# One transfer for the query weights, a projection in one part, and fillers ahead of it, in a decode kernel with attention and an MLP

## The chip, the cores and the metric

The kernel runs on one core of a Trainium2 chip. The metric is the device time of one execution in microseconds, lower is better. Four executions, spread over four kernels, were about a microsecond longer at a mean granted TensorE clock of 0.978 in place of 1.0. Nothing is read from those, but two of them count as fast by the rule used here and widen the interval of their run; the text says where. The profile's span is about 1.4 us shorter than the time.

## The reference

One token goes through a layer norm, then through two branches that are added to it: an attention with 32 query heads and 8 key/value heads over the last 4096 positions of a cache, and a small gated MLP with a sigmoid gate on its result.

```python
xn = layernorm(x)                                   # 1 x 512
q  = (xn @ wq).reshape(32 heads, 128)               # wq 512 x 4096, 4 MB
k, v = the last 4096 of 65536 positions, 8 heads    # 8 MB each
o  = softmax(q k^T * 128**-0.5) v                   # 4 query heads share one k/v head
A  = o.reshape(4096) @ wo                           # wo 4096 x 512, 4 MB
r  = sigmoid(xn @ w_r)
B  = xn + r * ((silu(xn @ w_gate) * (xn @ w_up)) @ w_down)   # 3 x 1.75 MB
out = x + A + B
```

All in all 30.67 MB are read once for one row of output.

## The kernel before

Each engine has a program of its own, ordered by semaphores. In the profile PE is TensorE, DVE is VectorE, ACT is ScalarE, POOL is GpSimd, and SP is SyncE, which here only issues transfers. All large transfers are issued on SP's queue, in this order: wq in two halves, k, v, gate, up, wo, down (in four pieces). `early` puts an issue ahead of the kernel's opening barrier. The weights are laid out so that each partition reads `kt` consecutive rows of wq: a half is 16 KB per partition, the whole 32 KB.

```python
    wq_sb = nc.alloc_sbuf_tensor("wq_sb", [P, KT, NQ], BF16)      # 128 x 4 x 4096
    KH = KT // 2
    wq_v = A_wq.rearrange("(p kt) n -> p kt n", kt=KT)
    ...
    t_wq = [early(nc.sync, "wq0", wq_sb[:, 0:KH, :], wq_v[:, 0:KH, :])]
    t_x = early(nc.scalar, "x", xrow[:], ...)
    ...
    t_wr = dma(ac, "wr", wr_row[:], ...)                          # 1 KB, on ACT's queue
    t_wq.append(dma(sy, "wq1", wq_sb[:, KH:, :], wq_v[:, KH:, :]))
```

`warm(n)` is n matmuls of zeros, 128 x 512, meant to keep TensorE's clock up; `fill(n)` is 2n of them. `gf` is the MLP's gate factor, spread to all partitions by a small matmul. The q projection is done in two parts, one for each half of wq, each with 16 matmuls in four column groups at a time (by the trace the second half's start in fours within 10 ns, and the fours are 0.215 us apart):

```python
    warm(2)
    PE.need(t_gf, t_ones)
    t_gfp = PE.mark(te.matmul(ps[:, 6, 264:265], lhsT=ones_f[0:1, :], rhs=sml[:, 4:5], ...))
    ...
    for kh in range(2):
        if kh == 1:
            for ch in range(2):                                   # clears the banks of the scores
                te.matmul(sc[:, ch, :], lhsT=zst[:], rhs=zmov[:], start=True, stop=False, ...)
            warm(1)
        PE.need(t_wq[kh], t_ps0)
        for hf in range(2):
            for kt in range(kh * KH, (kh + 1) * KH):
                for c in range(4):
                    ins = te.matmul(ps[32 * c:32 * c + 1, hf, :], lhsT=xnT[:, kt:kt + 1],
                                    rhs=wq_sb[:, kt, (4 * hf + c) * 512:(4 * hf + c + 1) * 512],
                                    start=(kt == 0), stop=(kt == KT - 1), tile_position=(0, 32 * c))
            if kh == 1:
                ...                                               # ACT evicts q
```

Then q is transposed, ten fillers run, and the loop over the eight k heads begins: DVE copies a head's k, TensorE transposes it, DVE and ACT evict it, TensorE multiplies it by q. Softmax, the product with v, and the gate and up projections follow, then 24 fillers, the wo matmuls, and those of down:

```python
    with te.Fori(0, 12):
        fill(1)
    PE.need(t_oT2)
    for k, (j0, j1) in enumerate(wo_chunks):                      # one transfer, 32 matmuls
        PE.need(t_wo[k])
        ...
    for k, (j0, j1) in enumerate(wd_chunks):                      # four transfers, 28 matmuls
        PE.need(t_wd[k])
        ...
```

Of the kernel before, what the change touches and what calls it, by code (L numbers as in the profile page):

```python
# [38 lines left out]
def kernel(  # L39
# [14 lines left out]
    nc = tc.nc  # L54
    P = 128
    D = A_x.shape[2]
    KT = D // P
# [15 lines left out]

    wq_sb = nc.alloc_sbuf_tensor("wq_sb", [P, KT, NQ], BF16)
    xrow = nc.alloc_sbuf_tensor("xrow", [1, D], BF16)
    KH = KT // 2
    wq_v = A_wq.rearrange("(p kt) n -> p kt n", kt=KT)

    ahead, ends_at = {}, {}
# [23 lines left out]
    def early(eng, name, out_, in_):  # L103
        s = nc.alloc_semaphore("d_" + name)
        ins = eng.dma_start(out=out_, in_=in_)
        ins.then_inc(s, 16)
        ahead[ins.ins.name] = ins.ins.engine
        return (s, 16)

    t_wq = [early(nc.sync, "wq0", wq_sb[:, 0:KH, :], wq_v[:, 0:KH, :])]  # L110
    t_x = early(nc.scalar, "x", xrow[:], A_x.rearrange("a b d -> (a b) d"))
    W3, F1, F2, F3 = 2, 2, 1, 1

# [13 lines left out]
    q4 = sb("q4", [P, 2, 512], BF16)  # L127
# [8 lines left out]
    zst = sb("zst", [P, P], BF16)  # L136
    zmov = sb("zmov", [P, 512], BF16)
# [14 lines left out]
    xnT = sb("xnT", [P, KT], BF16)  # L152
# [11 lines left out]
    ps = nc.alloc_psum_tensor("ps", [P, 8, 512], F32)  # L164
    psf = ps[:].rearrange("p a b -> p (a b)")
    tp = ps[:, 0:4, :].bitcast(BF16)
    sc = ps[:, 4:6, :]
# [17 lines left out]
    PE, ACT, DVE, POOL, SP = (Eng(nc, nc.tensor, "pe"), Eng(nc, nc.scalar, "act"), Eng(nc, nc.vector, "dve"),  # L185
                              Eng(nc, nc.gpsimd, "pool"), Eng(nc, nc.sync, "sp"))
    te, ac, ve, gp, sy = nc.tensor, nc.scalar, nc.vector, nc.gpsimd, nc.sync

    def warm(n):
        for _ in range(n):  # L190
            te.matmul(ps[:, 7, :], lhsT=zst[:], rhs=zmov[:], start=True, stop=True)  # L191

    def fill(n):
        warm(2 * n)

    def ends(ins):
        ends_at[ins.ins.engine] = ins.ins.name
        return ins

    def dma(eng, name, out_, in_):  # L200
        s = S("d_" + name)
        ins = eng.dma_start(out=out_, in_=in_)  # L202
        ins.then_inc(s, 16)
        if name == "v0":
            ends(ins)
        return (s, 16)

    t_wr = dma(ac, "wr", wr_row[:], B_w_r.rearrange("(a d) -> a d", a=1))
    t_wq.append(dma(sy, "wq1", wq_sb[:, KH:, :], wq_v[:, KH:, :]))
    TP = W // PH  # L210

    def pair(name, tile_, cache, i0, i1):
# [22 lines left out]
    t_ps0 = DVE.mark(ve.memset(ps[:, 0:2, :].rearrange("p a b -> p (a b)"), 0.0))  # L235
# [17 lines left out]
    for kt in range(KT):  # L253
        ins = te.matmul(ps[:, 6, 256 + kt:257 + kt], lhsT=xn_row[:].rearrange("a (p k) -> a k p", k=KT)[:, kt, :],  # L254
                        rhs=ident_bf[0:1, 0:1], start=True, stop=True)
# [9 lines left out]
    t_identf = DVE.mark(ve.tensor_copy(out=ident_f[:], in_=ident_bf[:]))  # L265
    DVE.need(t_rth)
    t_gf = DVE.mark(ve.tensor_scalar(out=sml[:, 4:5], in0=sml[:, 3:4], scalar1=0.25, scalar2=0.25, op0=ALU.mult, op1=ALU.add))
    warm(2)
    PE.need(t_gf, t_ones)
    t_gfp = PE.mark(te.matmul(ps[:, 6, 264:265], lhsT=ones_f[0:1, :], rhs=sml[:, 4:5], start=True, stop=True))  # L270
    with nc.allow_low_precision(reason="0/1 values are exact in bf16"):
# [4 lines left out]
                                     in_=ident_bf[:].rearrange("p (q h) -> p h q", h=2)))  # L276
# [11 lines left out]
    PE.need(t_xnT)  # L288
    t_qe = []
    t_qpad = []  # L290
    for kh in range(2):
        if kh == 1:
            for ch in range(2):
                te.matmul(sc[:, ch, :], lhsT=zst[:], rhs=zmov[:], start=True, stop=False, skip_group_check=True)
            warm(1)
        PE.need(t_wq[kh], t_ps0)
        for hf in range(2):
            for kt in range(kh * KH, (kh + 1) * KH):
                for c in range(4):
                    ins = te.matmul(ps[32 * c:32 * c + 1, hf, :], lhsT=xnT[:, kt:kt + 1],  # L300
                                    rhs=wq_sb[:, kt, (4 * hf + c) * 512:(4 * hf + c + 1) * 512],
                                    start=(kt == 0), stop=(kt == KT - 1), tile_position=(0, 32 * c))
            if kh == 1:
                t_qp = PE.mark(ins)
                ACT.need(t_qp)
                t_qe.append(ACT.mark(ac.copy(out=q4[:, hf, :], in_=ps[:, hf, :])))  # L306

    def q_out(hf, t_qt):
        DVE.need(t_qt, t_qpad0)
# [5 lines left out]
    for hf in range(2):  # L315
# [3 lines left out]
        for hl in range(4):  # L319
            ins = te.transpose(qT_ps[:, hl, :], q4[:, hf, hl * DH:(hl + 1) * DH], ident_bf[:])  # L320
# [76 lines left out]
    with te.Fori(1, 9) as i:  # L397
# [36 lines left out]
                              start=True, stop=True))  # L434
# [6 lines left out]
    for h in range(2):  # L441
        PE.need(t_p[h])
        for k in range(8):
            ins = te.transpose(tp[:, h, k * P:(k + 1) * P], p_sb[:, h, k * P:(k + 1) * P], ident_bf[:])
# [39 lines left out]
    with te.Fori(1, 9) as i:  # L484
# [4 lines left out]
        for tl in range(4):  # L489
            ins = te.matmul(pv_ps[32 * tl:32 * tl + 32, :], lhsT=pTcur[:, tl].rearrange("p q e r -> p (q e r)"),  # L490
                            rhs=vin[:, 0].rearrange("p (q t) d -> p t q d", t=4)[:, tl],
                            start=True, stop=False, tile_position=(0, 32 * tl))
        ins.then_inc(pe_pva, 1)
        te.wait_ge(s_vb, i)
        for tl in range(4):
            ins = te.matmul(pv_ps[32 * tl:32 * tl + 32, :], lhsT=pTcur[:, 4 + tl].rearrange("p q e r -> p (q e r)"),  # L496
                            rhs=vin[:, 1].rearrange("p (q t) d -> p t q d", t=4)[:, tl],
                            start=False, stop=True, tile_position=(0, 32 * tl))
        ins.then_inc(pe_pv, 1)
        collect(psf[:, bass.ds(4 * 512 + g * 8, 8)]).then_inc(pe_col, 1)  # L500
        for _ in range(W3):
# [10 lines left out]
                               in_=ps[:, 4, 8:72].rearrange("p (g u j) -> p g j u", g=HP, u=2), axis=AX.X))  # L512
# [7 lines left out]
    for m in range(2):  # L520
        PE.need(t_g if m == 0 else t_u)
        for kt in range(KT):
            for c in range(4):
                ins = te.matmul(ps[32 * c:32 * c + 1, 2 + m, 0:FC], lhsT=xnT[:, kt:kt + 1],
                                rhs=wgu[:, m * KT * F + kt * F + c * FC:m * KT * F + kt * F + (c + 1) * FC],
                                start=(kt == 0), stop=(kt == KT - 1), tile_position=(0, 32 * c))
# [18 lines left out]
    def grouped(j, lhsT, w):  # L545
        c = j % 4
        return te.matmul(a_ps[32 * c:32 * c + 1, :], lhsT=lhsT, rhs=w[:, j * D:(j + 1) * D], start=(j < 4), stop=False,  # L547
                         tile_position=(0, 32 * c), skip_group_check=True)

    def by_halves(lhsT, row, start=False, stop=False):  # L550
        for c in range(2):
            ins = te.matmul(g_ps[c], lhsT=lhsT, rhs=row[:, c * HD:(c + 1) * HD], start=start, stop=stop,  # L552
                            tile_position=(0, 32 * c), skip_group_check=True)
        return ins

    for k, (j0, j1) in enumerate(wo_chunks):
        PE.need(t_wo[k])
        for j in range(j0, j1):
            ins = grouped(j, oT2[:, j:j + 1], wo_sb)
# [4 lines left out]
    for k, (j0, j1) in enumerate(wd_chunks):  # L564
        PE.need(t_wd[k])
        for j in range(j0, j1):
            ins = by_halves(hTr[:, j, 0:1], wd_sb[:, j * D:(j + 1) * D], start=(j == 0), stop=(j == FB - 1))
# [42 lines left out]
```

## Time and profile before

| | before |
|---|---|
| time, median of 3 runs | 78.77 us (78.75 to 78.80) |
| span of the profiled run | 77.4 us |
| TensorE, VectorE, ScalarE busy | 73%, 57%, 39% of the span |
| moved from memory | 30.67 MB, 397 GB/s over the span |

The question is which wait ends last. A line of the timeline gives the start in us, how long the group lasted, the engine, the source line, the operation with output and inputs, how many instructions were merged, and in brackets the idle time ahead of it and what ended that.

A second source is used throughout: the trace's records of single DMA packets, each with start, duration and size. The page counts 16 DMA engines, and each of the large transfers has 16 completion writes of 4 bytes in the records (272 for the 17 of the kernel before); I read them as one from each engine when its share is done. The last of the 16 is taken as the landing (for wo in the kernel before it is at 70.52 us, the last of the 16 updates of its semaphore at 70.97, and PE starts at 71.11); the time from the first to the last is called the spread here.

### The profile page before, as it was taken

The page shows a single profiled execution, that of the slowest core. Times are in us where ns is not written, and L with a number is a line of the kernel's source. Part 1 is how long each engine was busy: PE and PEld are TensorE (multiplying, and loading weights), DVE is VectorE, ACT ScalarE, POOL GpSimd, SP SyncE. Part 2 cuts the span into 40 slices and gives each one's busy share as a digit, 9 for nine tenths or more (in the row PEclk, how much of TensorE's full clock was granted, in tenths as well). Part 3 has the DMA queues.
Part 4 walks back from the last instruction along what each step waited for, and adds up shares of the span by engine and source line. Part 5 has one row for each costly group of instructions (what it writes and reads, how often), then busy time and mean ns, then how long its engine had stood idle before and what let it go on. Part 6 is the DMA issues. An engine that isn't in the chain of part 4 may idle for free.

```text
span 77.4 us, 1658 instructions
## 1 busy us (share of the span) xinstructions
PE 56.4 (73%) x634; PEld 29.9 (39%) x652; DVE 43.8 (57%) x96; ACT 30.3 (39%) x41; POOL 10.2 (13%) x22
## 2 busy tenths in 40 slices
PE   0015965676997997997995766788887798872891
PEld 0010411335775685685682225222232254431340
DVE  2764900109956957966963672987989347400212
ACT  2771002301895896797775044333333420000001
POOL 3950000000230210220217700000000000000000
PEclk9999999999999999999999999999999999999999
DMA  5999999999999999999999999999999979969910
GB/s 128 398 416 407 441 457 449 407 415 407 466 449 415 415 415 441 457 441 407 411 415 441 457 432 407 415 451 385 467 385 489 516 305 542 441 291 400 361 41 1
DMA packets 2457, 30.72 MB, mean 397 GB/s; under 512 B 275, under 2 KB 406, under 8 KB 790
## 3 DMA queue, kind: packets, MB, share of 16 engines
q1 hardware_dynamic: 2450, 30.67, 94.0%
q8 instruction: 2, 0.03, 0.2%
q14 instruction: 1, 0.01, 0.0%
q10 hardware_dynamic: 4, 0.00, 0.0%
HBM read 30.67 MB, written 0.00 MB: 397 GB/s over the span
## 4 chain that ended last, share of the span: by engine, by line
DMA 71%; PE 13%; ACT 8%; DVE 3%; issue 1%; SPq 1%
DMA k_sb<-in_B_w_down_dram 51%; DMA k_sb<-in_A_k_cache_dram 20%; ACT kT L352 8%; PE ps L380 7%; PE ps L552 3%; PE ps L389 2%; DVE kin L344 2%; DVE kT L349 1%; SPq L202 1%; DVE kT L575 1%; SPq L84 0%; SPq L101 0%
## 5 line engine op out<-in xcount | busy, mean ns | idle before, releaser
L352 ACT COPY kT<-ps 128x1024 bf16<-128x1024 bf16 x19 | 18.5, 1016 | 9.4 <-PE ps L380 9.4
L380 PE MATMUL ps<-perm_bf,kin 128*128 128x128 bf16 x256 | 17.0, 220 | 1.3 <-DVE kin L344 0.9
L380 PEld LDWEIGHTS ps<-perm_bf,kin 128*128 128x128 bf16 x256 | 14.3, 98 | 5.6 <-issue 4.2
L344 DVE COPY kin<-k_sb 128x2048 bf16<-128x2048 bf16 x16 | 11.0, 690 | 5.4 <-DMA k_sb<-in_A_k_cache_dram 4.7
L191 PE MATMUL ps<-zmov,zst 128*128 128x512 bf16 x27 | 9.9, 397 | 2.3 <-PEq L84 1.2
L349 DVE COPY kT<-ps 128x1024 bf16<-128x1024 bf16 x13 | 9.0, 689 | 2.6 <-PE ps L380 2.2
L475 ACT CAST pvS<-ps 128x512 bf16<-128x512 f32 x8 | 4.7, 585 | 10.0 <-PE ps L481 10.0
L389 PE MATMUL ps<-kT,qAB 128*32 128x512 bf16 x68 | 6.8, 389 | 1.9 <-ACT kT L352 1.9
L337 POOL COPY qAB<-qpad 128x64 bf16<-128x64 bf16 x8 | 3.8, 471 | 31.7 <-PE ps L389 31.7
L191 PEld LDWEIGHTS ps<-zmov,zst 128*128 128x128 bf16 x45 | 4.0, 98 | 5.7 <-issue 2.1
L455 DVE COPY vin<-v_sb 128x2048 bf16<-128x2048 bf16 x8 | 5.5, 684 | 1.1 <-PE ps L490 1.0
L461 DVE COPY vin<-v_sb 128x2048 bf16<-128x2048 bf16 x8 | 5.5, 682 | 0.0
L490 PE MATMUL ps<-vin,pTcur 128*32 128x512 bf16 x32 | 3.2, 386 | 2.6 <-ACT pvS L475 2.2
L576 ACT CAST kT<-ps 1x256 bf16<-1x256 f32 x1 | 0.4, 362 | 11.8 <-PE ps L552 11.8
L502 PE MATMUL ps<-zmov,zst 128*128 128x512 bf16 x16 | 4.7, 376 | 0.0
L562 DVE TENSOR_TENSOR kT<-ps,kT 128x512 f32<-128x512 f32 x1 | 0.7, 692 | 6.4 <-PE ps L547 6.4
L254 PE MATMUL ps<-ident_bf,xn_row 1*128 1x1 bf16 x4 | 0.3, 166 | 5.2 <-DVE xn_row L249 5.2
L300 PE MATMUL ps<-wq_sb,xnT 128*1 128x512 bf16 x32 | 2.9, 500 | 1.4 <-DMA wq_sb<-in_A_wq_dram 1.4
L496 PE MATMUL ps<-vin,pTcur 128*32 128x512 bf16 x32 | 3.2, 387 | 0.3 <-DVE vin L461 0.2
L490 PEld LDWEIGHTS ps<-vin,pTcur 128*32 128x32 bf16 x32 | 1.1, 92 | 6.0 <-DVE vin L455 5.5
L389 PEld LDWEIGHTS ps<-kT,qAB 128*32 128x32 bf16 x68 | 1.9, 92 | 3.9 <-DVE kT L349 1.1
L306 ACT CAST q<-ps 128x512 bf16<-128x512 f32 x2 | 1.1, 588 | 5.5 <-PE ps L300 5.5
(92 smaller groups left out, 51.7 us busy)
## 6 DMA issues: line engine op xcount, KB each, us to landing
k_sb<-in_A_k_cache_dram SPq DMA_DIRECT2D x4, 2048.0 KB, 22.6
v_sb<-in_A_v_cache_dram SPq DMA_DIRECT2D x4, 2048.0 KB, 38.4
wq_sb<-in_A_wq_dram SPq DMA_DIRECT2D x2, 2048.0 KB, 9.3
k_sb<-in_A_wo_dram SPq DMA_DIRECT2D x1, 4096.0 KB, 37.7
wq_sb<-in_B_w_gate_dram SPq DMA_DIRECT2D x1, 1792.0 KB, 43.5
wq_sb<-in_B_w_up_dram SPq DMA_DIRECT2D x1, 1792.0 KB, 47.4
k_sb<-in_B_w_down_dram SPq DMA_DIRECT2D x1, 896.0 KB, 39.5
k_sb<-in_B_w_down_dram SPq DMA_DIRECT2D x1, 512.0 KB, 40.3
```

The source lines that it names most:

```text
L191: te.matmul(ps[:, 7, :], lhsT=zst[:], rhs=zmov[:], start=True, stop=True)
L337: gp.tensor_copy(out=qAB[:], in_=qpad[:, g]).then_inc(s_q, 1)
L344: ve.tensor_copy(out=kin[:, 2 * h:2 * h + 2, :], in_=k_sb[:, g, 2 * h:2 * h + 2, :]).then_inc(s_c[h], 1)
L349: ve.tensor_copy(out=kT[:, b, :], in_=tp[:, b, :]).then_inc(s_ev[b], 1)
L352: ac.copy(out=kT[:, b, :], in_=tp[:, b, :]).then_inc(s_ev[b], 1)
L380: ins = te.transpose(tp[:, b, k * P:(k + 1) * P], kin[:, b, k * P:(k + 1) * P], perm_bf[:])
L389: ins = te.matmul(sc[32 * cq:32 * cq + 32, e, :], lhsT=qAB[:, e, :], rhs=kT[:, b, :].rearrange("d (k h q) -> d h k q", h=2, q=PH)[:, e], s ...
L455: ve.tensor_copy(out=vin[:, 0].rearrange("p (q k) d -> p q (k d)", q=4), in_=v_in[:, :, 0:4 * DH]).then_inc(s_va, 1)
L461: ve.tensor_copy(out=vin[:, 1].rearrange("p (q k) d -> p q (k d)", q=4), in_=v_in[:, :, 4 * DH:]).then_inc(s_vb, 1)
L475: ac.copy(out=pvS[:].rearrange("p t d -> p (t d)"), in_=pv_ps).then_inc(s_pvs, 1)
L490: ins = te.matmul(pv_ps[32 * tl:32 * tl + 32, :], lhsT=pTcur[:, tl].rearrange("p q e r -> p (q e r)"), rhs=vin[:, 0].rearrange("p (q t) d ...
L502: te.matmul(ps[:, 7, :], lhsT=zst[:], rhs=zmov[:], start=True, stop=True)
```

## The change

Its intent: load wq as one transfer with the larger pieces, do the whole projection behind it in one part, and use the time that PE now spends waiting for fillers, so that the projection runs at the full clock.

```diff
-    t_wq = [early(nc.sync, "wq0", wq_sb[:, 0:KH, :], wq_v[:, 0:KH, :])]
+    t_wq = early(nc.sync, "wq", wq_sb[:], wq_v)
...
-    t_wq.append(dma(sy, "wq1", wq_sb[:, KH:, :], wq_v[:, KH:, :]))
...
-    warm(2)
+    with te.Fori(0, 6):
+        fill(1)
     PE.need(t_gf, t_ones)
...
-    for kh in range(2):
-        if kh == 1:
-            for ch in range(2):
-                te.matmul(sc[:, ch, :], lhsT=zst[:], rhs=zmov[:], start=True, stop=False, skip_group_check=True)
-            warm(1)
-        PE.need(t_wq[kh], t_ps0)
-        for hf in range(2):
-            for kt in range(kh * KH, (kh + 1) * KH):
...
+    for ch in range(2):
+        te.matmul(sc[:, ch, :], lhsT=zst[:], rhs=zmov[:], start=True, stop=False, skip_group_check=True)
+    PE.need(t_wq, t_ps0)
+    for hf in range(2):
+        for kt in range(KT):
 ...                            # the matmuls and ACT's evictions of q, one level less deep
```

## The prediction

> **What bounds the kernel now.** I read the chain that ended last first, then the DMA row of the 40 slices, then the DMA issues, then PE's timeline at both ends of the run. The page of the kernel before, its chain and its DMA row:
>
> ```profile
> DMA  5999999999999999999999999999999979969910
> ...
> ## 4 chain that ended last, share of the span: by engine, by line
> DMA 71%; PE 13%; ACT 8%; DVE 3%; issue 1%; SPq 1%
> DMA k_sb<-in_B_w_down_dram 51%; DMA k_sb<-in_A_k_cache_dram 20%; ACT kT L352 8%; PE ps L380 7%; PE ps L552 3%; PE ps L389 2%; DVE kin L344 2%; DVE kT L349 1%; SPq L202 1%; DVE kT L575 1%; SPq L84 0%; SPq L101 0%
> ```
>
> The 51% is the wait for the down projection, which was issued at 33.6 us and landed at 73.2: it stands last in one queue that is never empty. The DMA row is at 9 from the second slice to slice 32. So the length is startup, plus 30.67 MB at the rate of the 16 DMA engines, plus a short tail. The queue order is wq, k, v, gate, up, wo, down; only the first entry is touched.
>
> The issues of the same page (KB each, us from issue to landing):
>
> ```profile
> wq_sb<-in_A_wq_dram SPq DMA_DIRECT2D x2, 2048.0 KB, 9.3
> k_sb<-in_A_wo_dram SPq DMA_DIRECT2D x1, 4096.0 KB, 37.7
> ```
>
> wq is two transfers. They were issued at 0.00 and 1.26 us, and the view of tile wq_sb gives 7.5 us for the shorter landing, so with a median of 9.3 the other took 11.1: they landed at 7.5 and 12.4. wo is already what wq is to become: 4 MB in one issue.
>
> PE's timeline at the start (start us, duration, operation, idle time before it and what ended it):
>
> ```profile
> 6.67 1.01 PE L191 MATMUL ps<-zmov,zst 128*128 128x512 bf16 x2 [1.23 <-PEq L84]
> 7.83 0.58 PE L270 MATMUL ps<-sml,ones_f 1*128 1x1 f32 x2
> 8.34 1.88 PE L300 MATMUL ps<-wq_sb,xnT 128*1 128x512 bf16 x16
> ...
> 12.41 1.03 PE L300 MATMUL ps<-wq_sb,xnT 128*1 128x512 bf16 x16 [1.44 <-DMA wq_sb<-in_A_wq_dram]
> ...
> 14.98 2.11 PE L191 MATMUL ps<-zmov,zst 128*128 128x512 bf16 x5
> 18.03 0.34 PE L380 MATMUL ps<-perm_bf,kin 128*128 128x128 bf16 x3 [0.95 <-DVE kin L344]
> ```
>
> The first half of q ran in 1.88 us, the second, of equal work, in 1.03. And the loop over k cannot start before 18.03, since it waits for DVE's copy of the first k transfer, with PE idle for 0.95 us. The same timeline at the end:
>
> ```profile
> 64.26 5.12 PE L191 MATMUL ps<-zmov,zst 128*128 128x512 bf16 x12
> 71.11 1.90 PE L547 MATMUL ps<-k_sb,oT 128*1 128x512 bf16 x32 [1.73 <-DMA k_sb<-in_A_wo_dram]
> ```
>
> Everything that PE has to do before the output projection is over at 64.2; it then runs 24 fillers (12 records are missing from the trace), idles for 1.73 us and starts when wo has landed. This is the slack of the whole compute side, 1.73 us.
>
> [...] wq's second half and the four k transfers land some 4.87 us apart per 2.097 MB, 431 GB/s. [...] the 16 completion writes of the first half of wq spread over 0.60 us. [...] the single matmul falls from about 0.61 us to 0.38 by 10.6 us, 3.9 us after PE's work began at 6.67. [...] The trace has two such packets on the instruction queue, at 22.6 and 74.3 us. Which engine's they are it does not show.
>
> **The change, part by part.**
>
> *The transfer.* I read single packets from the trace's packet records. wq is now 256 packets of 16 KB, which take 611 ns (median); as 32 KB pieces it is 128, and wo's 32 KB packets take 1218 ns. Per DMA engine that is 16 x 0.611 = 9.78 us against 8 x 1.218 = 9.74: **0.03 us saved**. SP issues one transfer less, 0.33 us, so k is issued at about 1.26 in place of 1.64; but k's packets stand behind wq's until about 11.4, so that is worth nothing. wq lands at 12.4 as before. The first half's landing at 7.5 has no use any more.
>
> *The q projection.* 32 matmuls in one run behind 12.41 in place of 16: at the warm pace 2 x 1.03 = 2.06 us, so it ends at 14.47 in place of 13.44, **1.03 us later**. All of the first-half work that hid behind the transfer now stands behind it.
>
> *The fillers.* warm(2) and warm(1), three matmuls, go; 12 come, from 6.67. Two cold ones took 1.01 us, of which the last one's own duration is 0.61, so the pace is some 0.4 us. Warm, 24 took 5.12 us, 0.213 each; that row also shows that the loop adds nothing. Estimate: cold until about 10.3 is 8 to 9 fillers, the other 3 or 4 take 0.8 us, end at 11.1. The gate's small matmul, 0.58, ends at 11.7, and the two that clear the score banks at 12.1. So PE stands ready some 0.3 us ahead of wq, and warm. If [...] all 12 are cold, it is 6.67 + 5.1 + 0.58 + 0.85 = 13.2, and q starts 0.8 us late. The gate's factor comes at 11.8 in place of 9.6; its first readers are the transposes of q at 14.5, so that is hidden.
>
> *What follows.* The second eviction of q on ACT (0.58 us) ends about 15.2, the transposes about 15.7, the ten fillers of the next loop (2.11 us) about 17.8. Before, they were through at about 17.1. The k loop waits for the copy that ends at 17.97 in any case: 0.7 or 0.8 of the 0.95 us of slack is used, and **the loop starts at 18.03 still**. Gate and up are issued 1.03 us later (14.5), into a queue that has 16 MB of k and v ahead of them; they land as before. The stream, wo's landing and the tail stay.
>
> Sum: 78.77 - 0.03 + 0 = **78.74 us**, that is, unchanged. The change puts work that was free behind a wait, and pays for it with slack.
>
> **Rivals.**
>
> *PE becomes late.* If q runs cold or the fillers are late by 0.8 us, the k loop starts some 0.7 to 1 us later. For it speaks that the change uses nearly all of the 0.95 us. Against it as a cost to the end: the second slack, 1.73 us before wo. Only more than that shows; 32 cold matmuls (3.76 us) would shift the loop by about 1.6 us and still just fit. Worth at most +0.3 us.
>
> *Larger pieces make the stream faster.* For it: 4 MB in half as many packets and one completion less. Against it: the two durations are proportional to 0.3%. Even a percent on 4 MB would be 0.1 us.
>
> *The slowest DMA engine changes.* This is the one I take seriously. Beside the instruction packet at 22.6 us, one data packet of 16 KB took 1.12 us, and another engine had 1.27 at 38.1 beside a small one; after the first the completion writes of each transfer spread over 1.72 us in place of 0.60, and keep that to the end. wo's last write comes at 70.52, the second last at 69.92, the third last at 69.38. So one late engine sets when wo is there. The change rearranges a few PE instructions (out: three matmuls with their loads; in: a loop of two)[...]. If the first packet went elsewhere or away, wo could land 0.6 us sooner, and 1.1 if the second did too; if it met the engine that is already late by 0.4 us more[...], up to 1 us later. Against it: the four loops of the kernel before, over 30 rounds, show only two fetches, and the instruction count hardly moves.
>
> **Range and chances.** Three runs of before lie within 0.05 us. The mechanism gives -0.03; a different chip or run, and the fetch, give perhaps half a microsecond either way: 78.2 to 79.2. Over 2% would be 1.6 us; no term above reaches that alone. Faster 0.03, same 0.94, slower 0.03.
>
> **What would show it.** wq as one issue with 32 KB packets near 1.22 us, landing at 12.3 to 12.5; the first k transfer at 17.2 to 17.3; q's 32 matmuls from 12.4 in about 2.06 us; the k loop from 18.0 to 18.2; idle time on PE before wo of 1.5 to 1.8 us; wo's matmuls from about 71.1. I am wrong if wo lands more than 0.3 us away from that (then look for the instruction packets and the spread of the completion writes), if q takes over 2.5 us (cold), or if the k loop starts after 18.5.

## The result

Six runs of the changed kernel gave a median of 78.86 us (five from 78.68 to 79.14, and one of 80.18 at the clock of 0.978); six of before gave 78.82 (78.75 to 78.98). Executions over 1.5% slower than the fastest of the same kernel are left out of the means. A ratio here is the mean time of one kernel's fast runs over that of the other's in the same rounds, so not quite the ratio of the medians. It is 1.0003, with a 95% interval from 0.9979 to 1.0026. In a later group, six more runs gave 78.85 against 78.76, ratio 1.0009 (0.9992 to 1.0025). **Nothing moved.**

The page of the changed kernel: its DMA row, its chain, its issues.

```profile
DMA  9697989999999999999999999999999989979910
...
DMA 72%; PE 14%; ACT 6%; DVE 3%; issue 2%; SPq 0%
...
wq_sb<-in_A_wq_dram SPq DMA_DIRECT2D x1, 4096.0 KB, 12.6
k_sb<-in_A_wo_dram SPq DMA_DIRECT2D x1, 4096.0 KB, 37.4
```

The DMA row has a 6 and a 7 among the first four slices and is at 8 or 9 from there to slice 35, the chain is still 72% waiting for transfers, and wq lands at 12.6 us in place of 12.4. PE's timeline at the start:

```profile
6.79 4.03 PE L190 MATMUL ps<-zmov,zst 128*128 128x512 bf16 x12 [1.36 <-PEq L83]
10.76 0.38 PE L269 MATMUL ps<-sml,ones_f 1*128 1x1 f32 x2
11.07 0.61 PE L291 MATMUL ps<-zmov,zst 128*128 128x512 bf16 x2
12.65 1.90 PE L296 MATMUL ps<-wq_sb,xnT 128*1 128x512 bf16 x32 [0.98 <-DMA wq_sb<-in_A_wq_dram]
14.48 0.40 PE L315 MATMUL ps<-ident_bf,q 128*128 128x128 bf16 x4
15.32 0.38 PE L315 MATMUL ps<-ident_bf,q 128*128 128x128 bf16 x4 [0.44 <-ACT q L301]
15.54 2.32 PE L190 MATMUL ps<-zmov,zst 128*128 128x512 bf16 x10
18.25 0.96 PE L375 MATMUL ps<-perm_bf,kin 128*128 128x128 bf16 x14 [0.38 <-DVE kin L339]
```

PE waits 0.98 us for wq with the clock up, does all of q in 1.90 us, and still waits 0.38 us for the first k copy. Of the 0.95 us of idle time that stood here before, 0.57 are used. At the other end:

```profile
64.42 5.34 PE L190 MATMUL ps<-zmov,zst 128*128 128x512 bf16 x24
71.16 1.90 PE L542 MATMUL ps<-k_sb,oT 128*1 128x512 bf16 x32 [1.40 <-DMA k_sb<-in_A_wo_dram]
```

The wo matmuls start at 71.16 in place of 71.11. The idle time ahead of them went from 1.73 to 1.40 us. Together with the 0.05 us by which wo's matmuls began later, the compute side did get 0.38 us later, and it did not matter.

### The profile page after: what moved, and what is told of

Same layout as the page of the kernel before. It is cut to its first block, busy times and chain, and to the rows that moved or that the text cites. A ratio compares the mean times of both kernels' runs of the same rounds, so it can differ in the third digit from the quotient of the medians.

```text
span 77.4 us, 1706 instructions
## 1 busy us (share of the span) xinstructions
PE 59.0 (76%) x661; PEld 30.9 (40%) x661; DVE 44.1 (57%) x96; ACT 30.4 (39%) x41; POOL 10.3 (13%) x22
## 4 chain that ended last, share of the span: by engine, by line
DMA 72%; PE 14%; ACT 6%; DVE 3%; issue 2%; SPq 0%
DMA k_sb<-in_B_w_down_dram 51%; DMA k_sb<-in_A_k_cache_dram 21%; PE ps L375 8%; ACT kT L347 6%; PE ps L547 3%; PE ps L384 3%; DVE kin L339 2%; DVE kT L344 1%; DVE kT L570 1%; SPq L201 0%; SPq L83 0%; SPq L100 0%
## 5 line engine op out<-in xcount | busy, mean ns | idle before, releaser
L190 PE MATMUL ps<-zmov,zst 128*128 128x512 bf16 x54 | 13.9, 408 | 1.4 <-PEq L83 1.4
L190 PEld LDWEIGHTS ps<-zmov,zst 128*128 128x128 bf16 x54 | 5.1, 103 | 7.9 <-issue 4.0
L497 PE MATMUL ps<-zmov,zst 128*128 128x512 bf16 x16 | 4.7, 376 | 0.0
L455 DVE COPY pTcur<-ps 128x256 bf16<-128x256 bf16 x8 | 2.3, 285 | 1.6 <-PE ps L439 1.6
## 6 DMA issues: line engine op xcount, KB each, us to landing
wq_sb<-in_A_wq_dram SPq DMA_DIRECT2D x1, 4096.0 KB, 12.6
```

Source lines behind the costliest of these rows:

```text
L190: te.matmul(ps[:, 7, :], lhsT=zst[:], rhs=zmov[:], start=True, stop=True)
L497: te.matmul(ps[:, 7, :], lhsT=zst[:], rhs=zmov[:], start=True, stop=True)
```

## The experiments

The theory: the end is set by the bytes in the queue and by the slowest DMA engine; everything that PE does before wo's landing has slack, and the change spends slack. The rivals are those of the prediction: PE becomes late; the size of the pieces sets the speed of the stream; instruction packets shift the slowest engine.

One table first, since a single number sorts the runs. "Last write" is the last completion write of the down projection, from the packet records; the last column is the span less that.

| run | time, us (runs) | ratio to before in the same group (95%) | first 16 KB instruction packet, us | wo: last write (spread) | last write | span less last write |
|---|---|---|---|---|---|---|
| before | 78.77 (3) | | 22.6 | 70.52 (1.76) | 74.96 | 2.41 |
| changed | 78.86 (6) | 1.0003 (0.9979 to 1.0026) | 23.9 | 70.56 (1.98) | 75.00 | 2.42 |
| changed, again | 78.85 (6) | 1.0009 (0.9992 to 1.0025) | 23.7 | 70.42 (1.71) | 74.86 | 2.41 |
| no fillers | 79.00 (4) | 1.0014 (0.9988 to 1.0040) | 31.5 | 70.88 (2.11) | 75.31 | 2.41 |
| fillers alone | 78.88 (4) | 1.0040 (0.9973 to 1.0107) | 22.6 | 70.55 (1.75) | 74.99 | 2.41 |
| 12 rounds | 79.21 (4) | 1.0021 (0.9969 to 1.0073) | 32.9 | 70.49 (1.80) | 74.93 | 3.03 |
| 20 rounds | 82.05 (4) | 1.0422 (1.0384 to 1.0460) | 27.5 | 70.51 (1.91) | 74.95 | 5.19 |
| no up weights | 74.46 (4) | 0.9449 (0.9432 to 0.9466) | 29.9 | 66.25 (1.80) | 70.69 | 2.40 |
| pieces of 8 KB | 79.86 (4) | 1.0126 (1.0102 to 1.0150) | 24.9 | 71.50 (2.18) | 76.03 | 2.41 |
| fewer PE instructions | 83.50 (6) | 1.0593 (1.0566 to 1.0620) | 29.9 | 70.51 (1.92) | 74.96 | 7.73 |
| loops written out | 78.97 (4) | 1.0053 (1.0000 to 1.0105) | 22.1 | 70.59 (1.95) | 75.03 | 2.41 |
| the same, longer | 79.06 (4) | 1.0049 (1.0024 to 1.0074) | 22.8 | 70.72 (2.09) | 75.16 | 2.40 |
| DVE padded | 78.76 (1) | | 30.5 | 70.49 (1.80) | 74.94 | 2.41 |

In ten of thirteen profiles the span ends 2.40 to 2.42 us after the last piece of the down projection has landed, whatever was done to PE. The other three are those in which PE comes too late, and say by how much.

### The fillers undone

```diff
-    with te.Fori(0, 6):
-        fill(1)
+    warm(2)
```

> The changed kernel with its six rounds of fillers undone (two fillers as before), so the transfer and the one-part q alone. Theory (the DMA stream sets the end, PE has slack): PE idles over 3 us ahead of wq, the 32 matmuls of q run cold in 3.5 to 3.9 us in place of 1.90, the k loop starts at 20 to 21 us in place of 18.25, most or all of it hidden in the 1.40 us of idle time ahead of wo and in the waits for k: time 78.8 to 79.4. Rival (PE is late and it shows in full): +2 us or more, 80.8. wq's last completion write near 12.3, as in the changed kernel, if the 32 KB pieces are what moved it from 12.05.

Measured: 79.00 us. PE's timeline of this run:

```profile
12.47 3.58 PE L295 MATMUL ps<-wq_sb,xnT 128*1 128x512 bf16 x32 [2.79 <-DMA wq_sb<-in_A_wq_dram]
...
19.50 1.06 PE L374 MATMUL ps<-perm_bf,kin 128*128 128x128 bf16 x16
...
71.50 1.90 PE L541 MATMUL ps<-k_sb,oT 128*1 128x512 bf16 x32 [0.52 <-DMA k_sb<-in_A_wo_dram]
```

After 2.79 us of idling, q takes 3.58 us in place of 1.90, and the k loop starts 1.25 us later (at 19.50, a little earlier than I expected). All of it is hidden: PE still waits 0.52 us for wo. That wo's matmuls start at 71.50 is the stream's doing, its last write came at 70.88 in this execution. So the fillers do what they are for, and in this kernel nothing hangs on it yet. The landing of wq, 12.09 us here by the packets, did not repeat the 12.28 of the changed kernel's first profile.

### The fillers alone

```diff
 # in the kernel before, wq in two transfers
-    warm(2)
+    with te.Fori(0, 6):
+        fill(1)
```

> The kernel before with the six rounds of fillers alone; wq in two transfers, q in two parts. Theory: both q parts warm (about 1.03 us each), the first from 11.1 to 12.2, k loop at 18.03, time as before within 0.3 us (78.8). wq's last completion write at 12.05, spread 0.60, if the pieces set it and not the order of PE's work. Rival that the fillers themselves gain or cost: over 0.4 us away.

Measured: 78.81, 78.67, 78.95 and one run of 79.75 at the granted clock of 0.978; it carries the wide interval. Both halves of q took 1.03 us, from 11.68 and 13.40, and the k loop started at 18.02. wq's last write came at 11.87, with a spread of 0.36, where I had expected before's 12.05 and 0.60. With two executions of 16 KB pieces (11.87, 12.05) and ten of 32 KB (11.80 to 12.28) the landings overlap: **beside the scatter of the stream's start, no effect of the size of the pieces shows.**

### Twelve and twenty rounds

```diff
-    with te.Fori(0, 6):
+    with te.Fori(0, 12):      # and 20
         fill(1)
```

> The changed kernel with 12 rounds of fillers in place of 6: 12 more fillers at 0.213 us, 2.56 us. Theory with the slacks read from its trace: 0.98 us of idle time ahead of q, 0.38 ahead of the k loop, so the loop starts at 19.3 to 19.6; then 1.40 us ahead of wo, of which 0 to 0.5 us remains. Time 78.8, within 0.3 us of the changed kernel. Rival (PE bound): +1.2 us or more.

> The changed kernel with 20 rounds of fillers: 28 more, 5.97 us. Theory: the three slacks (0.98 + 0.38 + 1.40 = 2.76 us) are used up, and perhaps 0.5 us more in waits for the second k transfer; k loop at 22.6 to 23, wo's matmuls 2.7 to 3.2 us later, no idle time ahead of them, time 81.4 to 82.1. If the tail hides more (wd is then all there when PE comes to it), up to 0.7 us less.

The two timelines, 12 rounds and then 20:

```profile
6.79 8.09 PE L190 MATMUL ps<-zmov,zst 128*128 128x512 bf16 x24 [1.36 <-PEq L83]
...
72.25 1.90 PE L542 MATMUL ps<-k_sb,oT 128*1 128x512 bf16 x32
```

```profile
6.80 10.43 PE L190 MATMUL ps<-zmov,zst 128*128 128x512 bf16 x40 [1.36 <-PEq L83]
...
69.16 5.34 PE L190 MATMUL ps<-zmov,zst 128*128 128x512 bf16 x24
74.43 1.90 PE L542 MATMUL ps<-k_sb,oT 128*1 128x512 bf16 x32
```

With 12 rounds it is a near thing: 79.38, 79.19, 79.24 and 78.49 us, undecided by its interval. I had expected PE to be just in time, with the k loop from 19.3 to 19.6; in the profiled run, the one of 79.38, the loop began at 20.81 and PE was late (no idle time ahead of wo, and wo's data there since 70.49). The reason is in the first line: 24 fillers took 8.09 us. At 0.213 us each, the 12 extra ones should have added 2.56 us to the 4.03 of the changed kernel; they added 4.06. The cold stretch was longer in this execution. In the changed kernel's first profile the fillers start 0.427 us apart up to 9.31 us, and 0.216 apart from 9.59 on. With a cold filler at twice the warm 0.213, the 12 or 24 of a run give an estimate of the cold stretch (after some 0.17 us are taken off for the last one, which takes 0.38 itself): 2.6 us in the changed kernel's first profile, 5.6 here, or about 6 and 13 fillers. The trace's own clock records, which some of the profiles have and this one has not, agree with such estimates: the full clock is on record from 9.43 us in the changed kernel's first profile, 2.64 after its fillers began, and from 10.14 with 20 rounds, 3.34 after, where the fillers give 3.3. In the seven profiles that have such records it is 2.6 to 4.1 us after the first filler.

With 20 rounds the slack is gone and PE sets the end: wo's matmuls start 3.27 us later than in the changed kernel, the time is 82.05 us, 3.2 more. This is just past the upper end of what was expected (2.7 to 3.2 for wo), and so is the k loop, at 23.16 where I had 22.6 to 23. The stream does not care: its last write is at 74.95. So **the slack is real**, but its size moves with the cold stretch. The 28 extra fillers, 5.97 us at the warm pace, took 6.40 us more than the twelve of the changed kernel's first profile and 5.58 more than those of its second (4.85), and wo's matmuls came 3.27 and 3.42 us later: what was hidden is 3.1 us by the one and 2.2 by the other.

### Bytes taken away

```diff
-    t_u = dma(sy, "u", wgu[:, KT * F:2 * KT * F], B_w_up.rearrange("(p kt) f -> p (kt f)", kt=KT))
+    t_u = t_g
...
-                                rhs=wgu[:, m * KT * F + kt * F + c * FC:m * KT * F + kt * F + (c + 1) * FC],
+                                rhs=wgu[:, kt * F + c * FC:kt * F + (c + 1) * FC],
...
-    with te.Fori(0, 12):
+    with te.Fori(0, 3):
         fill(1)
```

The result is wrong: the gate weights stand in for the up weights.

> The changed kernel without the transfer of the up weights (the gate weights are used twice: the result is wrong on purpose, the instructions of PE are the same), and with 3 rounds of fillers in place of 12 ahead of wo, so that PE is ready at about 65.7. Theory (the bytes in the queue and the slowest DMA engine set the end): each DMA engine carries 8 packets of 14 KB fewer, 8 x 0.539 = 4.31 us; wo's last completion write at 66.2 to 66.3, time 78.85 - 4.3 = 74.5, at most 0.4 us off. Rival (compute is the bound and the stream only keeps pace with it): wo's data come earlier and wait, 77 us or more.

Measured: 74.46 us, against 74.5 expected. The timeline of this run:

```profile
63.99 1.46 PE L190 MATMUL ps<-zmov,zst 128*128 128x512 bf16 x6
66.85 1.90 PE L542 MATMUL ps<-k_sb,oT 128*1 128x512 bf16 x32 [1.40 <-DMA k_sb<-in_A_wo_dram]
69.03 0.93 PE L547 MATMUL ps<-k_sb,hTr 128*1 128x256 bf16 x14 [0.28 <-DMA k_sb<-in_B_w_down_dram]
```

PE's work before the last fillers ends at 64.0 us, in place of 64.4, and still the kernel is 4.4 us faster, because 1.8 MB fewer stand in the queue. (The 18 fillers had to go so that PE would not be the next bound; with 1.40 us of idle time behind them they could not have been the gain.) This is what shows the bound, where the profile alone only suggests it: shifting PE's work at the front moved nothing, and taking bytes out gained all of their time.

### Pieces of 8 KB

```diff
-    t_wq = early(nc.sync, "wq", wq_sb[:], wq_v)
+    t_wq = early(nc.sync, "wq", wq_sb[:, 0:1, :], wq_v[:, 0:1, :])
...
+    t_wqs = [dma(sy, f"wq{j}", wq_sb[:, j:j + 1, :], wq_v[:, j:j + 1, :]) for j in range(1, KT)]
...
-    PE.need(t_wq, t_ps0)
+    PE.need(t_wq, t_ps0, *t_wqs)
```

> The changed kernel with wq in four transfers of 8 KB pieces, q in one part behind all four. Packets of 14, 16 and 32 KB in the trace fit 37.1 ns per KB and 7 to 9 ns per packet. Theory: 24 packets more per DMA engine than with 32 KB, 0.2 us on wq's landing at most, lost in the run-to-run spread of its start; time 78.8 to 79.1. Rival (the size of the pieces sets the speed of the stream): 8 KB pieces cost several per cent of 9.7 us, 0.4 us or more.

Measured: 79.86 us, a whole microsecond slower, and **my expectation was wrong**. wq landed at 13.18 us by the packets. The stretches of 2 us from 3 to 9, for the changed kernel and then for this one (after the stretch and its length come the busy time and count of PE, its weight loads, DVE, ACT and POOL, then the granted clock, the DMA engines' mean busy share and GB/s):

```profile
3.00:5.00 2.00, 0.00 (x0) 0.00 (x0) 1.57 (x4) 1.55 (x2) 1.89 (x3) 1.00 1.08 459
5.00:7.00 2.00, 0.47 (x5) 0.34 (x6) 0.22 (x3) 0.23 (x2) 0.00 (x0) 1.00 1.14 492
7.00:9.00 2.00, 2.00 (x6) 0.68 (x5) 1.87 (x10) 0.20 (x1) 0.00 (x0) 1.00 0.77 328
```

```profile
3.00:5.00 2.00, 0.00 (x0) 0.00 (x0) 1.51 (x4) 1.55 (x2) 2.00 (x3) 1.00 0.98 353
5.00:7.00 2.00, 0.26 (x4) 0.21 (x4) 0.16 (x1) 0.23 (x2) 0.03 (x1) 1.00 0.95 328
7.00:9.00 2.00, 1.10 (x3) 0.40 (x4) 1.09 (x6) 0.20 (x1) 0.00 (x0) 1.00 1.01 406
```

A packet counts here in the stretch in which it starts, so that a single stretch is coarse. Over all 6 us the stream ran at 362 GB/s (the mean of 353, 328 and 406) in place of 426, and in place of the 418 of the kernel before with its 16 KB pieces, and never got the difference back. The packet records say what the cost is not. The median packet of 8 KB took 309 ns, about half of the 611 of one of 16 KB. But 58 of the 512 took over 1.2 times the median. With larger pieces it is 14 to 18, and nearly all of those are among the first 16 packets of the stream. Summed up, wq's packets take 11.04 us per engine, against 10.35 to 10.55 in ten profiles with 32 KB and 10.32 and 10.48 in two with 16 KB. That is about 0.6 us. The mean of wq's 16 completion writes came 0.8 us later (12.47 us, against 11.62 to 11.72 in the other twelve), and the rest of the microsecond is unevenness: a spread of 1.20 us, against 0.33 to 0.97. Why packets stall here stays open. The run doubled the number of transfers, from the two of the kernel before to four, together with halving the pieces, and which of the two did it is not separated. The small size alone does not: of the 128 packets of 7 KB in the down projection, none took over 1.2 times their median of 274 ns. For the change itself this is the reading: what was lost with 8 KB pieces is a matter of stalls more than of a constant per packet, at two transfers of 16 KB it does not show, and going on to 32 KB gained nothing.

PE was late here as well (its program resumed at 7.90 us in place of 6.79), but it idled 1.53 us ahead of wo, so the microsecond is the stream's.

A small transfer beside the full queue came at different times too. The 1 KB of w_r, issued at 1.20 us on the other queue, completed at 4.15 us in this run, at 5.97 and 6.10 beside 16 KB pieces, at 6.62 to 7.02 beside 32 KB. In the kernel before, the first instruction on DVE that reads w_r began at 6.67 us, and by the profile its wait was ended by PE's sequencer. In the changed kernel it waited for w_r:

```profile
6.97 0.68 DVE L258 SCALAR_TENSOR_TENSOR rprod<-xn_row,wr_row 1x512 f32<-1x512 bf16 x1 [1.34 <-DMA wr_row<-in_B_w_r_dram]
```

### The changed kernel again

> The changed kernel again, unedited, for the spread of its runs and a second profile beside the other three of this group. Theory: ratio to before 0.998 to 1.003; q warm (1.9 us); wq's last completion write anywhere from 11.9 to 12.3, since so far this moved between executions of the same transfers. If the pieces of 32 KB set it, 12.28 again.

Measured: 78.85 us (78.69 to 79.01). wq's last write at 12.19, k loop at 18.14, idle time ahead of wo 1.36 us; the twelve fillers took 4.85 us this time.

### Fewer PE instructions

The next three are about the third rival. In all thirteen profiles two packets of 16 KB appear on an instruction queue. After the first one, the spread of the completion writes of every transfer goes from 0.3 to 1.3 us up to 1.6 to 2.3, and stays there up to wo (in the kernel before from 0.60 to 1.72; beside the second one, at 74.34 us there, PE's timeline shows no gap).

```diff
-    W3, F1, F2, F3 = 2, 2, 1, 1
+    W3, F1, F2, F3 = 2, 0, 0, 0
...
-        for k in range(8):
-            ins = te.transpose(tp[:, h, k * P:(k + 1) * P], p_sb[:, h, k * P:(k + 1) * P], ident_bf[:])
+        with te.Fori(0, 7) as k:
+            te.transpose(tp[:, h, bass.ds(k * P, P)], p_sb[:, h, bass.ds(k * P, P)], ident_bf[:])
+        ins = te.transpose(tp[:, h, 7 * P:8 * P], p_sb[:, h, 7 * P:8 * P], ident_bf[:])
```

> The changed kernel with 21 fewer PE instructions (543 in place of 564, counting each matmul with its load as two): the 16 transposes of the softmax in two loops, and the eight fillers of the softmax left out. Theory (the instruction packet at 74.4 us is PE's, and delays the last pieces of the down projection on one DMA engine): if these 21 take PE's end in front of the point where the packet is asked for, the packet is gone, the last completion write comes at 74.0 to 74.4 in place of 75.0, and the time falls by 0.3 to 0.5 us, to 78.4. If the point lies still further ahead, packet and time stay (78.8). Rival (the packet is not PE's, or does not matter to the end): packet gone or not, 78.8. The compute side gets at most 0.5 us later and is hidden by the 1.40 us ahead of wo.

Measured: 83.50 us. A miss, for a reason that I had not thought of. PE's timeline inside the new loop:

```profile
47.66 0.28 PE L439 MATMUL ps<-ident_bf,kin 128*128 128x128 bf16 x1 [0.22 <-issue]
48.22 0.28 PE L439 MATMUL ps<-ident_bf,kin 128*128 128x128 bf16 x1 [0.27 <-issue]
48.74 0.29 PE L439 MATMUL ps<-ident_bf,kin 128*128 128x128 bf16 x1 [0.23 <-issue]
```

A transpose whose address is in a register, in a loop of one, comes every 0.52 us; written out, eight took 0.62 us together. The stage with the two loops took 7.5 us in place of 1.4, all of it with the granted clock at a half. The trace tells which of the two edits halved the clock: it is at 1.00 from 42.0 to 43.8 us and at 0.50 from 43.9 to 60.8, so it fell over 3 us before the first transpose of the loops (47.16), in the idle time that the missing fillers had left (1.32 us up to 44.00; the changed kernel, with its fillers there, idles 0.36 us up to 44.31 at a clock of 1.00). What the loops cost at the full clock no run shows. PE was so late that the end is its own. The second instruction packet did not go away; it came at 78.6 us, 1.6 us after wo's matmuls had begun. The stream was untouched by all this: last write at 74.96, as before. So this run tells once more that the stream does not follow PE, and it answers nothing about the packet.

### Loops written out

```diff
-    with te.Fori(0, 6):
-        fill(1)
+    fill(6)
 ...                            # the loops of 5 and of 12 rounds likewise
```

In the longer version the 24 fillers ahead of wo are also replaced by 48 of half the width:

```diff
-    fill(12)
+    for _ in range(48):
+        te.matmul(ps[:, 7, 0:256], lhsT=zst[:], rhs=zmov[:, 0:256], start=True, stop=True)
```

> The changed kernel with its three loops of fillers written out: the same work, 65 more PE instructions (629). Theory: [...] the second instruction packet comes at 71 to 73 us in place of 74.4; wo has landed by then, so wo's matmuls stay at 71.1; down's pieces on that engine land later; time 78.6 to 79.2. Rival (instruction packets are not PE's): packet at 74.4.

> As the last, and the 24 fillers ahead of wo are 48 of half the width: same time on PE, 113 more PE instructions than the changed kernel (677). Theory: the second packet comes at 65 to 68 us, ahead of wo's landing. If it hits the DMA engine that is late already (both packets stand on one queue), wo's last completion write comes at 71.3 to 72.0 in place of 70.5 and the time rises by 0.8 to 1.3 us, to 79.6 to 80.1. If it hits another engine, this one gets no later than the late one (under 70.6) and the time stays at 78.8. Rival (packets of instructions are nothing to the stream): 78.8 with the packet early.

Measured: the second packet came at 67.74 us in the first and at 67.80 in the second, in place of 74.4. It moves with PE's program, so it is PE's (in the first I had expected it at 71 to 73, after wo's landing). It fell into wo's transfer, and wo's last write came at 70.59 and 70.72, against 70.42 and 70.56 in the two profiles of the changed kernel. The spread did not grow over it: 1.95 at the transfer before and 1.95 at wo in the first, 2.09 and 2.09 in the second. So it did not hit the late engine. And the down projection's last write stayed where it was, at 75.03 and 75.16, though the packet that I had blamed for its lateness was no longer there. **What keeps the last pieces late is then a delay from earlier in the stream, carried to the end**, and the rise of the spread after the first packet is the large one on record. The ratios are 0.5% over 1 in both. The first interval touches 1 and holds a run at the clock of 0.978; without that run the mean is 0.1% over before's. The second clears 1, and its profile has the last write 0.2 us later than before's. I read no more from it.

### DVE padded

```diff
+    pad = nc.alloc_sbuf_tensor("pad", [1, 32], F32)
+    for i in range(32):
+        ve.memset(pad[:, i:i + 1], 0.0)
```

> The changed kernel with 32 tiny memsets more on DVE, in its idle time ahead of q (227 instructions in place of 195). Looks only at the first instruction packet, at 22 to 33 us in the runs so far. If DVE asks for it, it comes some 32 of DVE's instructions sooner, before 16 us; if another engine does, it stays between 22 and 33 us. The time stays at 78.8 either way, since the late DMA engine keeps its delay to the end whenever it gets it.

One look: 78.76 us. The first packet of 16 KB came at 30.5, so by this test, one run, it is not DVE's. But an 8 KB packet on another instruction queue, which stood at 37.8 to 43.5 us in all other runs, came at 15.97: that one is DVE's. It delayed an engine as well (the spread of the next transfer rose from 0.71 to 1.20), and again the end did not move, since a later engine sets it.

Who asks for the first packet is open. It came between 22 and 33 us, at different places in the k loop for the same program: 23.9 and 23.7 us in the two profiles of the changed kernel, where the loop began at 18.2, but 32.9 with 12 rounds, which has the same instructions with another count in the loop. No run was without it, so its cost to the end (in the kernel before, the slowest engine is about 1.1 us behind where the 0.6 of the start had left it) is read from the spread and is not shown by a run that lacks it.

## Why the prediction was right

*The bound.* Shown. Bytes taken out moved the end by their full time (4.4 us measured, 4.2 to 4.3 in the last write, 4.3 worked out); 1.25 us of delay to the k loop moved nothing; and the span ends 2.40 to 2.42 us behind the last completion write in ten profiles, wherever PE stood.

*The transfer, 0.03 us.* Too small to see. PE had wq at 12.65 us where I had said 12.3 to 12.5, and the first k copy began at 17.49 where I had said 17.2 to 17.3; by the packets, wq landed within the scatter of the start, 11.80 to 12.28 us for the same 32 KB pieces, which is over ten times the term. The 32 KB packets took 1.22 us as said.

*The q projection.* It ran warm, in 1.90 us where I had 2.06. I had doubled 1.03; but 1.03 ends with the last matmul's own 0.38 us, against 0.215 from one four to the next, and that excess does not double. The pace of 16 matmuls is nearer 0.87 (1.90 less 1.03).

*The fillers.* Twelve took 4.03 us, ending at 10.8 where I had 11.1, and 4.17 to 5.28 in the other profiles with twelve. The bad case that I gave, all cold and q late, nearly occurred in the longer version: 5.28 us, q at 12.73 with no wait. It was harmless, as said.

*The slack.* Right in kind, and mis-sized by some tenths. The k loop began at 18.25 and 18.14 (18.0 to 18.2 said), because the first k copy was later by the start's scatter. The idle time ahead of wo was 1.40 and 1.36 us where I had said 1.5 to 1.8: the loop's 0.22 us had become 0.38 by the gate projection. I had put no loss there.

*The rivals.* "PE becomes late" holds only beyond some 2 to 3 us of slack (12 rounds at the edge, 20 beyond it). I had said that cold matmuls "would shift the loop by about 1.6 us and still just fit"; it was 1.25 and fitted. "Larger pieces make the stream faster" does not show between 16 and 32 KB. Four transfers of 8 KB pieces were slower, which I did not see in the median durations; whether by the pieces or by the number of transfers stays open. "The slowest DMA engine changes": the fact behind it stands, the conclusion does not. The first packet moved by up to 11 us from run to run and the second by 6.6 with the program, and wo's landing stayed within 70.42 to 70.88 in all runs but the two that changed the stream itself. And the weight that I gave to a few PE instructions more or less was misplaced: the first packet came at 23.9 us in the changed kernel and at 32.9 with 12 rounds, which has the same instructions.

## What to carry to other kernels

Before moving work on an engine, find out how far the span ends behind the last landing. Where that distance is the same whatever the engine does (here 2.40 to 2.42 us in ten of thirteen profiles), look for the gain in the stream, as here, where 1.8 MB less in the queue gained 4.4 us; idle time on the engine is then currency that costs nothing to spend until it is gone. Measure the slack by spending it, with fillers in steps, and the bound by removing bytes, even at the price of a wrong result. And a per-packet constant read from median durations did not tell what four transfers of 8 KB pieces cost (0.2 us at most expected for wq's landing, 1.0 us measured in the time): look at the stretch in GB/s and at the packets that stalled.
